# Sliding-window attention and SwiGLU on one core: the opening taken chunk by chunk, and x transposes two steps behind AV

## The chip, the cores and the metric

The kernel runs on one core of one Trainium2 chip. The metric is the device time of one execution in microseconds. Runs of the kernel before on the same chip stand beside every variant's runs, and all ratios are variant over before. PE is TensorE (matmul), PEld its weight load, ACT ScalarE, DVE VectorE, POOL GpSimd, SP SyncE. "Granted clock" is the share of full speed that the throttle gave to PE.

## The reference

```python
def _attn_ref(q, k, v):                      # B, H, S, D = 8, 8, 576, 64
    scores = (1.0 / np.sqrt(D)) * np.matmul(q, k.transpose(0, 1, 3, 2))
    rel = pos[:, None] - pos[None, :]
    scores = np.where((rel >= 0) & (rel < 64), scores, -1e9)   # window of 64, causal
    ...                                      # softmax over keys, then attn @ v
def reference(...):
    x = attn_out.transpose(0, 2, 1, 3).reshape(B * S, H * D)   # 4608 tokens x 512
    g = x @ w_gate; val = x @ w_val                            # 512 x 1536 each
    return (g * sigmoid(g) * val) @ w_out                      # 4608 x 512
```

## The kernel before

Tokens go in 36 chunks of 128. For a chunk n the steps are: transposes of k and q (`Tpe` on PE, `T` by DMA), scores and exponentials (`S`), attention times V (`AV`, with a division on VectorE that writes the tile `xb`), and the transpose of the result into `xT` (`X`, on PE, or by DMA if no engine is named). Four chunks make a group of 512 tokens. `F(c, f)` is one of the 12 blocks of gate and value matmuls of group c, optionally only columns lo to hi; `O(c, u)` is the output matmul of one chunk. V is needed twice, once shifted by 64 tokens across partitions: `shift_v` makes `vb` from `va`, either with two copies on an engine or with DMAs on SP's queue.

In every timeline below an engine's instructions stand in the order of these calls, and each waits for the semaphores of its inputs and buffers. So the order of the calls is each engine's queue. The kernel uses eight PSUM banks (the memory that PE writes to): `f` banks for F, one `o` bank for O, and `a` banks for the rest, each kind taken in rotation.

```python
    def opening(self):
        W = lambda a, b: (self.load_w("g", a, b), self.load_w("v", a, b))
        self.first_loads()                 # k and q of chunks 0, 1: one DMA each, on SP's and ACT's queue
        self.init()
        self.load(0, "v"); self.load(1, "v"); self.load(2, "kq")
        W(0, 1)
        self.load(2, "v"); self.load(3, "kqv")
        W(1, 2); W(2, 4); W(4, 6); ...
        self.warm(11)                      # dummy matmuls
        ... # casts and transposes of chunks 0 and 1 together
        self.S(0, True); self.S(1, True)
        self.shift_v(0, "dve"); self.shift_v(1, "dve")
        self.AV(0); self.Tpe(2, ("dve", "act")); self.AV(1)
        self.X(0, "act"); self.X(1, "dve")
        self.F(0, 0, 0, 256)
        self.banks("a", [5, 6, 7, 4])
        self.S(2, True); self.shift_v(2, "dve"); self.Tpe(3, ("dve", "act"))
        ...
        self.F(0, 1, 0, 256); self.AV(2)
        self.S(3, True); self.shift_v(3, "dve")
        self.F(0, 2, 0, 256); self.X(2, "act")
        self.F(0, 3, 0, 256); self.AV(3)
        self.F(0, 4, 0, 256); self.F(0, 5, 0, 256); self.X(3, "act")
        for f in range(6):
            self.F(0, f, 256, 512)
```

The softmax here doesn't subtract the row's maximum and nothing guards it: scores larger than these inputs give would overflow.

Of the kernel before, what the change touches and what calls it, by code (L numbers as in the profile page):

```python
# [17 lines left out]
BF = dt.bfloat16  # L18
# [131 lines left out]
class _Kernel:  # L150
# [15 lines left out]
    def alloc(self):  # L166
# [33 lines left out]
        f4 = lambda a: a.bitcast(F32).rearrange("p (h j d) -> p h j d", h=H, j=2)  # L200
        self.fk, self.fq = f4(hT[1][:, 0:2048]), f4(hT[1][:, 2048:4096])
        h1 = lambda a: [("hT", 1, f) for f in range(4 * a, 4 * a + 4)]
        self.fkk, self.fqk = h1(0), h1(1)
        c4 = lambda t: t[:, :].bitcast(BF).rearrange("p (j h d) -> p j h d", j=2, h=H)
        self.ck, self.cq = c4(self.ost[0]), c4(self.ost[1])
        self.ckk, self.cqk = [("ost", 0)], [("ost", 1)]
# [31 lines left out]
    def init(self):  # L238
        g = self.g
        self.zero(self.wup[:, :], ["wup"])  # L240
        g.op("act", lambda e: e.activation(self.wup[:, :], self.wup[:, :], ACTF.Exp), writes=["wup"])
        self.zero(self.ident[:, :], ["ident"])
        self.init_ident(self.ident, "ident")
        self.zero(self.wz[:, :], ["wz"])
        self.init_va(0, 4)
        self.zero(self.kT[:, :, 0:64], [("kT", -1, 0), ("kT", -1, 1)])
        self.zero(self.vb[0][0:64, :, 0:66], [("vb", 0, 0)])
        self.init_mask()
        for i in range(self.NP):
            self.zero(self.pt[i][:, :, 64:128], [("pt", i, 0), ("pt", i, 1)])  # L250
        self.init_va(4, self.NV)
# [42 lines left out]
    def shift_v(self, n, eng="sp"):  # L294
# [12 lines left out]
        for d, a, rk, wk in moves:  # L307
            if eng == "sp":
                g.op("sp", lambda e, d=d, a=a: e.dma_start(d, a), reads=rk, writes=wk, dma=True)
            else:  # L310
                self.copy(eng, d, a, rk, wk)
# [117 lines left out]
    def first_loads(self):  # L429
        for eng, x, dst, src, keys in (("sp", "k", self.fk, self.k, self.fkk), ("act", "q", self.fq, self.q, self.fqk)):  # L430
            d = dst.rearrange("p h j d -> p h (j d)")
            a = src[0, :, 0:256, :].rearrange("h (p j) d -> p h (j d)", j=2)
            self.g.op(eng, lambda e, d=d, a=a: e.dma_start(d, a), writes=keys, dma=True)

    def first_cast(self, x, eng, j):
        dst, src, keys, ck = (self.ck, self.fk, self.fkk, self.ckk) if x == "k" else (self.cq, self.fq, self.fqk, self.cqk)
        js = slice(j, j + 1) if j is not None else slice(0, 2)
        d = dst[:, js].rearrange("p j h d -> p h j d")
        wk = [("c", x, i) for i in range(2) if j in (None, i)]
        self.copy(eng, d, src[:, :, js], keys + ck, wk)  # L440

    def first_T(self, x, engs):
        g = self.g
        src = self.ck if x == "k" else self.cq
        for b in range(2):
            bank, bk = self.bank("a")
            tb = bank[:, 0:256].bitcast(BF).rearrange("p (c j t) -> p c j t", c=2, j=2)

            def pe(e, b=b, tb=tb):
                for j in range(2):  # L450
                    for c in range(2):
                        pr = 2 * b + c
                        r = e.transpose(tb[:, c, j, :], src[:, j, 2 * pr:2 * pr + 2, :], self.ident[:, :])
                return r

            rd = ["ident"] + [("c", x, j) for j in range(2)] + (self.ckk if x == "k" else self.cqk)
            g.op("pe", pe, reads=rd, writes=[bk])
            if x == "k":
                d = self.kT[:, 2 * b:2 * b + 2, 64:320]
                wk = [("kT", m, b) for m in (0, 1)]  # L460
            else:
                d = self.qT[:, 2 * b:2 * b + 2, 0:256]
                wk = [("qT", m, b) for m in (0, 1)]
            d = d.rearrange("p c (t j) -> p c t j", j=2)
            a = tb.rearrange("p c j t -> p c t j")
            self.copy(engs[b], d, a, [bk], wk)
# [66 lines left out]

    def hTk(self, ih):
        return [("hT", ih, f) for f in range(NF)] + [("hTp", ih, f, lo) for f in range(NF) for lo in (0, 256)]
# [46 lines left out]
    def opening(self):  # L582
        W = lambda a, b: (self.load_w("g", a, b), self.load_w("v", a, b))
        self.first_loads()
        self.init()
        self.load(0, "v")
        self.load(1, "v")
        self.load(2, "kq")
        W(0, 1)
        self.load(2, "v")  # L590
        self.load(3, "kqv")
        W(1, 2)
        W(2, 4)
        W(4, 6)
        self.load(4)
# [5 lines left out]

        self.banks("a", [0, 1, 2, 3, 5, 6, 7])
        self.warm(11)
        self.first_cast("k", "dve", None)
        self.first_cast("q", "act", 0)
        self.first_cast("q", "dve", 1)
        self.first_T("k", ("dve", "act"))
        self.first_T("q", ("dve", "act"))
        self.warm(2)
        self.S(0, True)  # L610
        self.S(1, True)
        self.shift_v(0, "dve")
        self.shift_v(1, "dve")
        self.AV(0)
        self.Tpe(2, ("dve", "act"))
        self.AV(1)
        self.X(0, "act")
        self.X(1, "dve")
        self.F(0, 0, 0, 256)
        self.banks("a", [5, 6, 7, 4])  # L620
        self.S(2, True)
        self.shift_v(2, "dve")
        self.Tpe(3, ("dve", "act"))
# [3 lines left out]
        self.load_wo(6, 12)  # L627
        for n in range(4, 8):
            self.shift_v(n)
        self.F(0, 1, 0, 256)  # L630
        self.AV(2)
        self.S(3, True)
        self.shift_v(3, "dve")
        self.F(0, 2, 0, 256)
        self.X(2, "act")
        self.F(0, 3, 0, 256)
        self.AV(3)
        self.F(0, 4, 0, 256)
        self.F(0, 5, 0, 256)
        self.X(3, "act")  # L640
        for f in range(6):
            self.F(0, f, 256, 512)
# [6 lines left out]
    def build(self):  # L649
        self.opening()  # L650
        self.Tpe(4, ("dve", "act"))
        self.F(0, 6)
        self.S(4)
        self.F(0, 7)
        self.AV(4)
        self.Tpe(5, ("dve", "act"))
        self.F(0, 8)
        self.X(4, "act")
# [3 lines left out]
        self.F(0, 10)  # L662
        self.X(5, "act")
        self.F(0, 11)
        self.Tpe(6, ("dve", "act"))
        self.Tpe(7, ("dve", "act"))
        for n in (8, 9, 10, 11):
# [3 lines left out]
        F1 = lambda *fs: [self.F(1, f, 0, 256) for f in fs]  # L671
        F1(0)
        self.S(6)
        F1(1, 2)
        self.AV(6)
        F1(3)
# [6 lines left out]
        self.X(7, "act")  # L683
        self.banks("a", [5, 6, 7])
        self.banks("o", [4])
        F1 = lambda *fs: [self.F(1, f, 256, 512) for f in fs]
        F1(0, 1)
        self.O(0, 0)
        self.S(8)
        self.load(12, after=8)  # L690
        F1(2, 3)
        self.AV(8)
        F1(4)
        self.O(0, 1)
        self.X(8, "act")
# [4 lines left out]
        self.AV(9)  # L700
        F1(7)
        self.X(9, "act")
# [3 lines left out]
        self.O(0, 2)  # L706
        self.AV(10)
        self.F(1, 8)
# [11 lines left out]
        self.O(0, 3)  # L720
# [66 lines left out]
```

## Time and profile before

| | before |
|---|---|
| time, median of 4 runs | 344.02 us (343.3 to 345.04) |
| span of the profiled run, granted clock | 341.6 us, 1.00 |
| first scores' mask matmul | 8.25 us |
| F behind x 3 starts | 25.0 us |
| scores of chunk 5 | 37.56 us |
| scores of chunk 13 | 92.70 us |

When PE reaches the scores of chunk 5, both versions have done exactly the same work: F(0,0) to F(0,8), chunks 0 to 4 through x, the transposes of chunk 5. The same holds at the scores of chunk 13. So differences there are pure gains or losses.

The view of busy time in stretches, of the kernel before; each engine has its busy us and count, and PEclk is the granted clock:

```profile
...
core 0: us, PE busy (x) PEld busy (x) DVE busy (x) ACT busy (x) POOL busy (x), PEclk, DMA share, GB/s
...
10.00:15.00 5.00, 3.45 (x63) 2.89 (x58) 2.99 (x11) 2.78 (x6) 5.00 (x7) 1.00 2.22 164
15.00:20.00 5.00, 4.73 (x77) 3.03 (x76) 4.03 (x12) 3.11 (x8) 5.00 (x8) 1.00 1.48 194
20.00:25.00 5.00, 4.08 (x52) 3.17 (x50) 4.75 (x14) 2.43 (x6) 5.00 (x8) 1.00 1.94 173
25.00:30.00 5.00, 5.00 (x46) 4.49 (x47) 4.19 (x10) 1.93 (x5) 5.00 (x8) 1.00 1.99 184
...
90.00:120.00 30.00, 30.00 (x251) 14.68 (x250) 20.78 (x45) 12.09 (x22) 8.26 (x10) 1.00 1.54 149
...
```

From 90 us on PE has no idle time. Whatever the change does must be done in the first 90 us.

The list of PE's waits of the kernel before, first from 5 to 25 us, then from 37 to 95 us ("x waits for y: us in total, times, longest"). L423 is the x transpose, L501 is F:

```profile
...
engine line waited for: us in total, times, longest us
PE ps L423 <- DVE xb L404: 1.0, 1, 1.0
...
PE ps L501 <- DVE uu L520: 0.7, 1, 0.7
PE ps L501 <- DVE xT L233: 0.5, 1, 0.5
PE ps L501 <- DMA Wv<-in_moe_w_val_dram: 0.5, 2, 0.3
...
```

```profile
...
PE ps L423 <- DVE xb L404: 2.3, 4, 1.3
PE ps L501 <- DVE uu L520: 0.7, 1, 0.7
...
```

In the opening no single wait exceeds 1.0 us. Later, most is 2.3 us that x transposes wait for `xb`, with AV's VectorE work just ahead of them.

How PE spends the time between the scores and AV of chunk 2, in its timeline (start, length, instruction):

```profile
...
15.46 0.41 PE L364 MATMUL ps<-qT,kT 64*128 64x64 bf16 x16
15.80 0.40 PE L477 MATMUL ps<-ident,kn 128*128 128x128 bf16 x4
...
16.35 0.61 PE L501 MATMUL ps<-xT,Wg 128*128 128x256 bf16 x4
16.92 0.61 PE L501 MATMUL ps<-xT,Wv 128*128 128x256 bf16 x4
17.37 0.19 PE L394 MATMUL ps<-vb,pt 128*128 128x65 bf16 x1
...
```

The scores (L364) start at 15.46 and AV (L394) at 17.37. The 1.9 us between them, in which ScalarE computes the exponentials, are filled with chunk 3's transposes (L477) and F(0,1).

### The profile page before, as it was taken

How to read it: one execution, taken by the hardware profiler on the slowest of the kernel's cores; microseconds unless marked ns; L12 is line 12 of the kernel's file. 1: busy time of each engine (PE TensorE's matmuls, PEld its weight loads, DVE VectorE, ACT ScalarE, POOL GpSimd, SP SyncE). 2: the span in 40 equal slices, each digit the busy share in tenths (PEclk: the TensorE clock that was granted, in tenths of full speed). 3: DMA queues.
4: the chain of work that ended last, by engine and by line, in shares of the span. 5: the costliest groups of instructions: out<-in, count | busy, mean ns of one | idle time of the engine just before them, and what ended most of it. 6: DMA issues, size and time to landing. Idle time of an engine off the chain costs nothing.

```text
span 341.6 us, 6841 instructions
## 1 busy us (share of the span) xinstructions
PE 330.3 (97%) x2705; PEld 172.2 (50%) x2705; DVE 222.5 (65%) x495; ACT 138.3 (40%) x252; POOL 111.8 (33%) x139
## 2 busy tenths in 40 slices
PE   7889998989999999999999999999999999999996
PEld 3567576654444444444444444444444444444444
DVE  8788987458666666666666666666666666655520
ACT  3555463355433333444333344444444443223221
POOL 8999760376322234333333334333300000000000
PEclk9999999999999999999999999999999999999999
DMA  9999999999999999999999999999953211100012
GB/s 177 172 183 185 182 207 159 173 194 200 183 152 143 140 146 145 142 145 141 141 140 136 153 138 139 131 141 141 129 141 93 76 48 46 49 31 33 31 59 96
DMA packets 174367, 44.93 MB, mean 132 GB/s; under 512 B 157888, under 2 KB 169856, under 8 KB 174336
## 3 DMA queue, kind: packets, MB, share of 16 engines
q0 software_dynamic: 118368, 18.36, 79.5%
q1 hardware_dynamic: 49744, 16.32, 29.2%
q10 hardware_dynamic: 6224, 9.83, 8.0%
q8 instruction: 21, 0.34, 0.5%
q14 instruction: 10, 0.08, 0.1%
HBM read 37.75 MB, written 9.44 MB: 138 GB/s over the span
## 4 chain that ended last, share of the span: by engine, by line
PE 86%; DVE 4%; POOL 3%; ACT 2%; DMA 2%; issue 1%; ACTq 0%; POOLq 0%
PE ps L501 50%; PE ps L547 27%; PE ps L364 3%; PE ps L394 2%; PE ps L395 2%; DMA Wv<-in_moe_w_val_dram 2%; DVE uu L520 2%; ACT pt L377 1%; POOL va L292 1%; DVE xb L404 1%; DVE hT L523 1%; PE ps L569 1%; POOL Wg L317 1%; PE ps L423 1%; POOL qn L292 1%
## 5 line engine op out<-in xcount | busy, mean ns | idle before, releaser
L520 DVE SCALAR_TENSOR_TENSOR uu<-sig,ps 128x512 bf16<-128x512 bf16 (+1 forms) x122 | 76.0, 623 | 86.7 <-ACT sig L512 85.9
L501 PE MATMUL ps<-xT,Wg 128*128 128x512 bf16 (+1 forms) x488 | 113.4, 355 | 1.9 <-DVE uu L520 1.4
L501 PE MATMUL ps<-xT,Wv 128*128 128x512 bf16 (+1 forms) x488 | 113.3, 355 | 0.5 <-DMA Wv<-in_moe_w_val_dram 0.5
L512 ACT ACTIVATE sig<-ps 128x512 bf16<-128x512 f32 (+1 forms) x122 | 66.9, 550 | 100.5 <-PE ps L501 100.5
L547 PE MATMUL ps<-Wo,hT 128*128 128x512 bf16 x420 | 96.1, 380 | 0.0
L523 DVE SCALAR_TENSOR_TENSOR hT<-uu,ps 128x512 bf16<-128x512 bf16 (+1 forms) x122 | 76.3, 626 | 4.2
L292 POOL DMA_DIRECT2D kn<-in_k_dram x38 | 33.4, 881 | 131.1 <-PE ps L364 126.3
L501 PEld LDWEIGHTS ps<-xT,Wv 128*128 128x128 bf16 x488 | 47.2, 98 | 47.2 <-DMA Wv<-in_moe_w_val_dram 0.8
L501 PEld LDWEIGHTS ps<-xT,Wg 128*128 128x128 bf16 x488 | 44.3, 98 | 40.6 <-ACT xT L231 1.7
L547 PEld LDWEIGHTS ps<-Wo,hT 128*128 128x128 bf16 x420 | 39.1, 98 | 44.5
L552 ACT ACTIVATE ost<-ps 128x512 f32<-128x512 f32 x35 | 20.9, 598 | 65.4 <-PE ps L547 65.4
L377 ACT ACTIVATE pt<-ps 128x512 bf16<-128x512 f32 x72 | 39.0, 596 | 18.7 <-PE ps L364 18.3
L292 POOL DMA_DIRECT2D va<-in_v_dram x40 | 35.7, 901 | 0.2 <-issue 0.2
L292 POOL DMA_DIRECT2D qn<-in_q_dram x38 | 33.6, 889 | 0.1
L404 DVE TENSOR_TENSOR xb<-ps,rc 128x256 bf16<-128x256 f32 x72 | 30.6, 425 | 2.5
L379 DVE TENSOR_TENSOR pt<-pt,mask 128x512 bf16<-128x512 bf16 x64 | 24.8, 420 | 8.0 <-ACT pt L377 7.5
L394 PE MATMUL ps<-vb,pt 128*128 128x65 bf16 x288 | 22.8, 193 | 0.4 <-DVE pt L379 0.2
L395 PE MATMUL ps<-va,pt 128*128 128x65 bf16 x288 | 22.8, 194 | 0.0
L394 PEld LDWEIGHTS ps<-vb,pt 128*128 128x128 bf16 x288 | 20.2, 98 | 4.6 <-DVE pt L379 1.2
L395 PEld LDWEIGHTS ps<-va,pt 128*128 128x128 bf16 x288 | 19.0, 97 | 3.3
L364 PEld LDWEIGHTS ps<-qT,kT 64*128 64x128 bf16 x576 | 10.4, 95 | 13.2 <-DVE rc L401 9.7
L364 PE MATMUL ps<-qT,kT 64*128 64x64 bf16 x576 | 14.7, 191 | 0.0
(47 smaller groups left out, 89.7 us busy)
## 6 DMA issues: line engine op xcount, KB each, us to landing
out_dram<-ost ACTq DMA_DIRECT2D x35, 256.0 KB, 4.9
vb<-va SPq DMA_DIRECT2D x63, 80.0 KB, 4.9
va<-in_v_dram POOLq DMA_DIRECT2D x32, 128.0 KB, 6.5
kn<-in_k_dram POOLq DMA_DIRECT2D x30, 128.0 KB, 4.5
qn<-in_q_dram POOLq DMA_DIRECT2D x30, 128.0 KB, 5.8
Wo<-in_moe_w_out_dram POOLq DMA_DIRECT2D x2, 768.0 KB, 14.9
Wg<-in_moe_w_gate_dram POOLq DMA_DIRECT2D x4, 256.0 KB, 7.0
Wv<-in_moe_w_val_dram POOLq DMA_DIRECT2D x4, 256.0 KB, 7.7
```

The lines of the kernel that those rows point to most:

```text
L292: self.g.op("pool", lambda e, d=d, a=a: e.dma_start(d, a), reads=gate, writes=ks, dma=True)
L364: r = e.matmul(sv[p][:, w, c], self.kT[ps, c, k0:k0 + 128], self.qT[ps, c, self.qs(n, 64 * w, 64 * w + 64)], start=not bias, stop=not bias ...
L377: g.op("act", lambda e, po=po, p=p: e.activation(po, sv[p], ACTF.Exp, scale=SCALE), reads=[bx[p][1]], writes=[pk])
L379: g.op("dve", lambda e, po=po: e.tensor_tensor(po, po, m, ALU.mult), reads=[pk, "mask"], writes=[pk])
L394: e.matmul(av[:, j, :], pt[:, h, 0:128], vb[:, h, 0:65], start=True, stop=False)
L395: r = e.matmul(av[:, j, :], pt[:, h, 64:192], va[:, h, 0:65], start=False, stop=True)
L404: g.op("dve", lambda e, xo=xo, av=av, rb=rb: e.tensor_tensor(xo, av[:, :, 0:64], rb, ALU.mult), reads=[bk, ("rc", ir)], writes=[("xb", ix, ...
L501: r = e.matmul(bank[:, lo:hi], W[:, kk, f * 128:f * 128 + 128], xT[:, kk, lo:hi], start=(kk == 0), stop=(kk == NK - 1))
L512: self.g.op("act", lambda e: e.activation(sig[:, lo:hi], G[:, lo:hi], ACTF.Tanh, scale=0.5), reads=[gk], writes=[("sig", i)])
L520: g.op("dve", lambda e: e.scalar_tensor_tensor(uu[:, lo:hi], sig[:, lo:hi], 1.0, G[:, lo:hi], ALU.add, ALU.mult), reads=[("sig", i), gk], ...
L523: g.op("dve", lambda e: e.scalar_tensor_tensor(hT[:, f, lo:hi], uu[:, lo:hi], 0.5, V[:, lo:hi], ALU.mult, ALU.mult), reads=[("uu", i), vk] ...
L547: r = e.matmul(OB[:, :], hT[:, f, 128 * u:128 * u + 128], self.Wo[:, f, :], start=(f == 0), stop=(f == NF - 1))
```

## The change

The intent: begin with chunk 0 alone instead of chunks 0 and 1 together, load V first, let ScalarE do V's shifts, hold W of F(0,1) back behind chunk 3, so that attention of the first chunks runs through early; and keep x transposes further behind AV. The diff, cut to its core:

```diff
 def init_...:
+        self.load(0, "v")                       # ahead of the identity matrix
-            self.zero(self.pt[i]...)            # all four on VectorE
+            # pt 0, 1 by copies on ScalarE, the rest on VectorE
-        self.init_va(4, self.NV)                # now at the end of the opening
 def opening:
-        self.first_loads()
+        self.first_loads(0); self.first_loads(1)       # a DMA per chunk for k and for q
...
         W(0, 1)
-        self.load(2, "v"); self.load(3, "kqv"); W(1, 2)
+        self.load(2, "vkq"); self.load(3, "vkq"); W(1, 2)
...
+        self.first_cast(0, "k", "dve"); self.first_cast(0, "q", "act")
+        self.Tpe(0, ("dve", "act")); self.warm(2); self.S(0, True)
+        self.first_cast(1, "k", "dve"); self.first_cast(1, "q", "dve")
+        self.shift_v(0, ("dve", "act")); self.Tpe(1, ("dve", "dve"))
+        self.AV(0)
+        self.S(1, True); self.shift_v(1, ("act", "act"))
+        self.X(0, "dve")
+        self.AV(1)
+        self.banks("a", [5, 6, 7, 4])
+        b0 = self.Fopen(); self.Fpart(b0, 0, 0, 0, 128)
+        self.Tpe(2, ("dve", "act")); self.X(1, "act")
+        self.Fpart(b0, 0, 0, 128, 256); self.Fclose(b0, 0, 0, 0, 256)
+        self.S(2, True); self.shift_v(2, ("act", "act")); self.shift_v(3)
+        self.AV(2)
+        self.Tpe(3, ("dve", "act"))
...
+        self.S(3, True); self.X(2, "dve")
+        self.F(0, 1, 0, 256); self.AV(3); self.F(0, 2, 0, 256); self.X(3, "act")
+        for f in range(3): self.F(0, f, 256, 512)
 def build:                                       # groups 0, 1
-        self.F(0, 10); self.X(5, "act"); self.F(0, 11)
-        self.Tpe(6, ...); self.Tpe(7, ...)
+        self.F(0, 10); self.Tpe(6, ...); self.X(5, "act"); self.F(0, 11)
...
-        F1(6, 7); self.X(7, "act"); ...; F1(0, 1); self.O(0, 0); self.S(8); F1(2, 3)
+        F1(6, 7); self.O(0, 0); self.X(7, "act"); self.O(0, 1); F1(0, 1, 2); self.S(8); F1(3)
         self.AV(8)
-        F1(4); self.O(0, 1); self.X(8, "act")
+        self.X(8); F1(4); self.O(0, 2)           # x 8 by DMA
...
         self.AV(9)
-        F1(7); self.X(9, "act"); self.S(10); self.O(0, 2); self.AV(10); self.F(1, 8)
+        self.X(9); F1(7); self.S(10); self.F(1, 8); self.AV(10); self.O(0, 3)   # x 9 by DMA
         self.X(10, "act")
```

More of the change, by code (lines that the diff above doesn't have):

```diff
@@ L199, in alloc @@
         self.ost = ring("ost", self.NO, DM, F32)
-        f4 = lambda a: a.bitcast(F32).rearrange("p (h j d) -> p h j d", h=H, j=2)
-        self.fk, self.fq = f4(hT[1][:, 0:2048]), f4(hT[1][:, 2048:4096])
-        h1 = lambda a: [("hT", 1, f) for f in range(4 * a, 4 * a + 4)]
-        self.fkk, self.fqk = h1(0), h1(1)
-        c4 = lambda t: t[:, :].bitcast(BF).rearrange("p (j h d) -> p j h d", j=2, h=H)
-        self.ck, self.cq = c4(self.ost[0]), c4(self.ost[1])
-        self.ckk, self.cqk = [("ost", 0)], [("ost", 1)]
+        f4 = lambda i: hT[1][:, 1024 * i:1024 * i + 1024].bitcast(F32)
+        self.fk, self.fq = [f4(0), f4(1)], [f4(2), f4(3)]
+        h1 = lambda i: [("hT", 1, 2 * i), ("hT", 1, 2 * i + 1)]
+        self.fkk, self.fqk = [h1(0), h1(1)], [h1(2), h1(3)]
         self.wup = sb("wup", 1, F32)
@@ L249, in init @@
         for i in range(self.NP):
-            self.zero(self.pt[i][:, :, 64:128], [("pt", i, 0), ("pt", i, 1)])
-        self.init_va(4, self.NV)
+            d, wk = self.pt[i][:, :, 64:128], [("pt", i, 0), ("pt", i, 1)]
+            if i < 2:
+                self.copy("act", d, self.wz[:, :].rearrange("p (h x) -> p h x", h=H), ["wz"], wk)
+            else:
+                self.zero(d, wk)
     def init_mask(self):
@@ L306, in shift_v @@
             moves.append((self.vb[i2][0:64], va[64:128], hi, [("vb", i2, 0)]))
-        for d, a, rk, wk in moves:
+        for j, (d, a, rk, wk) in enumerate(moves):
             if eng == "sp":
@@ L310, in shift_v @@
             else:
-                self.copy(eng, d, a, rk, wk)
+                self.copy(eng[j], d, a, rk, wk)
     def load_w(self, which, a, b):
@@ L427, in X @@
         self.copy(eng, xo, tb, [bk], [("xT", it, u)])
-    def first_loads(self):
-        for eng, x, dst, src, keys in (("sp", "k", self.fk, self.k, self.fkk), ("act", "q", self.fq, self.q, self.fqk)):
-            d = dst.rearrange("p h j d -> p h (j d)")
-            a = src[0, :, 0:256, :].rearrange("h (p j) d -> p h (j d)", j=2)
-            self.g.op(eng, lambda e, d=d, a=a: e.dma_start(d, a), writes=keys, dma=True)
-    def first_cast(self, x, eng, j):
-        dst, src, keys, ck = (self.ck, self.fk, self.fkk, self.ckk) if x == "k" else (self.cq, self.fq, self.fqk, self.cqk)
-        js = slice(j, j + 1) if j is not None else slice(0, 2)
-        d = dst[:, js].rearrange("p j h d -> p h j d")
-        wk = [("c", x, i) for i in range(2) if j in (None, i)]
-        self.copy(eng, d, src[:, :, js], keys + ck, wk)
@@ L442, in first_T, with first_loads @@
-    def first_T(self, x, engs):
-        g = self.g
-        src = self.ck if x == "k" else self.cq
-        for b in range(2):
-            bank, bk = self.bank("a")
-            tb = bank[:, 0:256].bitcast(BF).rearrange("p (c j t) -> p c j t", c=2, j=2)
-            def pe(e, b=b, tb=tb):
-                for j in range(2):
-                    for c in range(2):
-                        pr = 2 * b + c
-                        r = e.transpose(tb[:, c, j, :], src[:, j, 2 * pr:2 * pr + 2, :], self.ident[:, :])
-                return r
-            rd = ["ident"] + [("c", x, j) for j in range(2)] + (self.ckk if x == "k" else self.cqk)
-            g.op("pe", pe, reads=rd, writes=[bk])
-            if x == "k":
-                d = self.kT[:, 2 * b:2 * b + 2, 64:320]
-                wk = [("kT", m, b) for m in (0, 1)]
-            else:
-                d = self.qT[:, 2 * b:2 * b + 2, 0:256]
-                wk = [("qT", m, b) for m in (0, 1)]
-            d = d.rearrange("p c (t j) -> p c t j", j=2)
-            a = tb.rearrange("p c j t -> p c t j")
-            self.copy(engs[b], d, a, [bk], wk)
+    def first_loads(self, n):
+        for eng, dst, src, keys in (("sp", self.fk, self.k, self.fkk), ("act", self.fq, self.q, self.fqk)):
+            d = dst[n].rearrange("p (h d) -> p h d", h=H)
+            a = src[0, :, 128 * n:128 * n + 128, :].rearrange("h p d -> p h d")
+            self.g.op(eng, lambda e, d=d, a=a: e.dma_start(d, a), writes=keys[n], dma=True)
@@ L468, in Tpe, with first_cast @@
+    def first_cast(self, n, x, eng):
+        d, a, rk = (self.kn, self.fk, self.fkk) if x == "k" else (self.qn, self.fq, self.fqk)
+        self.copy(eng, d[n][:, :], a[n], rk[n], [(x + "n", n, 0), (x + "n", n, 1)])
     def Tpe(self, n, engs, what="kq"):
@@ L532, in F, with Fopen, Fpart, Fclose @@
         self.Fdve(c, f, i, G, gk, V, vk, lo, hi)
+    def Fopen(self):
+        return self.bank("f"), self.bank("f")
+    def Fpart(self, b, c, f, lo, hi):
+        self.Fmm(*b[0], self.Wg, "Wg", c, f, lo, hi)
+        self.Fmm(*b[1], self.Wv, "Wv", c, f, lo, hi)
+    def Fclose(self, b, c, f, lo, hi):
+        (G, gk), (V, vk) = b
+        i = self.Fact(G, gk, lo, hi)
+        self.Fdve(c, f, i, G, gk, V, vk, lo, hi)
     def hTk(self, ih):
@@ L583, in opening @@
         W = lambda a, b: (self.load_w("g", a, b), self.load_w("v", a, b))
-        self.first_loads()
+        self.first_loads(0)
+        self.first_loads(1)
         self.init()
-        self.load(0, "v")
         self.load(1, "v")
-        self.load(2, "kq")
         W(0, 1)
-        self.load(2, "v")
-        self.load(3, "kqv")
+        self.load(2, "vkq")
+        self.load(3, "vkq")
         W(1, 2)
-        W(2, 4)
+        W(2, 3)
+        W(3, 4)
         W(4, 6)
+        self.banks("a", [0, 1, 2, 3, 5, 6, 7])
+        self.warm(8)
+        self.first_cast(0, "k", "dve")
+        self.first_cast(0, "q", "act")
+        self.Tpe(0, ("dve", "act"))
+        self.warm(2)
+        self.S(0, True)
+        self.first_cast(1, "k", "dve")
+        self.first_cast(1, "q", "dve")
+        self.shift_v(0, ("dve", "act"))
+        self.Tpe(1, ("dve", "dve"))
+        self.AV(0)
+        self.S(1, True)
+        self.shift_v(1, ("act", "act"))
+        self.X(0, "dve")
+        self.AV(1)
+        self.banks("a", [5, 6, 7, 4])
+        b0 = self.Fopen()
+        self.Fpart(b0, 0, 0, 0, 128)
+        self.Tpe(2, ("dve", "act"))
+        self.X(1, "act")
+        self.Fpart(b0, 0, 0, 128, 256)
+        self.Fclose(b0, 0, 0, 0, 256)
+        self.S(2, True)
+        self.shift_v(2, ("act", "act"))
+        self.shift_v(3)
+        self.AV(2)
+        self.Tpe(3, ("dve", "act"))
         self.load(4)
@@ L600, in opening @@
         W(10, 12)
-        self.banks("a", [0, 1, 2, 3, 5, 6, 7])
-        self.warm(11)
-        self.first_cast("k", "dve", None)
-        self.first_cast("q", "act", 0)
-        self.first_cast("q", "dve", 1)
-        self.first_T("k", ("dve", "act"))
-        self.first_T("q", ("dve", "act"))
-        self.warm(2)
-        self.S(0, True)
-        self.S(1, True)
-        self.shift_v(0, "dve")
-        self.shift_v(1, "dve")
-        self.AV(0)
-        self.Tpe(2, ("dve", "act"))
-        self.AV(1)
-        self.X(0, "act")
-        self.X(1, "dve")
-        self.F(0, 0, 0, 256)
-        self.banks("a", [5, 6, 7, 4])
-        self.S(2, True)
-        self.shift_v(2, "dve")
-        self.Tpe(3, ("dve", "act"))
         self.load(6)
@@ L627, in opening @@
         self.load_wo(6, 12)
+        self.S(3, True)
+        self.X(2, "dve")
+        self.F(0, 1, 0, 256)
+        self.AV(3)
+        self.F(0, 2, 0, 256)
+        self.X(3, "act")
+        for f in range(3):
+            self.F(0, f, 256, 512)
+        self.init_va(4, self.NV)
         for n in range(4, 8):
             self.shift_v(n)
-        self.F(0, 1, 0, 256)
-        self.AV(2)
-        self.S(3, True)
-        self.shift_v(3, "dve")
-        self.F(0, 2, 0, 256)
-        self.X(2, "act")
-        self.F(0, 3, 0, 256)
-        self.AV(3)
-        self.F(0, 4, 0, 256)
-        self.F(0, 5, 0, 256)
-        self.X(3, "act")
-        for f in range(6):
-            self.F(0, f, 256, 512)
     def T8(self, n):
@@ L650, in build @@
         self.opening()
+        self.F(0, 3)
+        self.F(0, 4)
         self.Tpe(4, ("dve", "act"))
+        self.F(0, 5)
+        self.S(4)
         self.F(0, 6)
-        self.S(4)
+        self.AV(4)
         self.F(0, 7)
-        self.AV(4)
         self.Tpe(5, ("dve", "act"))
+        self.X(4, "act")
         self.F(0, 8)
-        self.X(4, "act")
         self.S(5)
@@ L662, in build @@
         self.F(0, 10)
+        self.Tpe(6, ("dve", "act"))
         self.X(5, "act")
         self.F(0, 11)
-        self.Tpe(6, ("dve", "act"))
+        F1 = lambda *fs: [self.F(1, f, 0, 256) for f in fs]
+        self.S(6)
+        F1(0, 1)
         self.Tpe(7, ("dve", "act"))
+        self.AV(6)
         for n in (8, 9, 10, 11):
@@ L670, in build @@
             self.T8(n)
-        F1 = lambda *fs: [self.F(1, f, 0, 256) for f in fs]
-        F1(0)
-        self.S(6)
-        F1(1, 2)
-        self.AV(6)
-        F1(3)
+        F1(2, 3)
         self.S(7)
@@ L682, in build @@
         F1(6, 7)
-        self.X(7, "act")
         self.banks("a", [5, 6, 7])
         self.banks("o", [4])
+        self.O(0, 0)
+        self.X(7, "act")
+        self.O(0, 1)
         F1 = lambda *fs: [self.F(1, f, 256, 512) for f in fs]
-        F1(0, 1)
-        self.O(0, 0)
+        F1(0, 1, 2)
         self.S(8)
         self.load(12, after=8)
-        F1(2, 3)
+        F1(3)
         self.AV(8)
+        self.X(8)
         F1(4)
-        self.O(0, 1)
-        self.X(8, "act")
+        self.O(0, 2)
         self.S(9)
@@ L700, in build @@
         self.AV(9)
+        self.X(9)
         F1(7)
-        self.X(9, "act")
         self.S(10)
@@ L705, in build @@
         self.T8(13)
-        self.O(0, 2)
+        self.F(1, 8)
         self.AV(10)
-        self.F(1, 8)
+        self.O(0, 3)
         self.X(10, "act")
@@ L719, in build @@
         self.load(17, after=12)
-        self.O(0, 3)
         self.F(1, 11)
```

## The prediction

> **What bounds the kernel now.** From about 84 us on PE is gapless: the view of busy time in stretches shows 20.00 us of PE in every 20 us at clock 1.00, the list of waits no PE wait after 100 us. So only the time up to 84 us can change. In the timeline real work on PE starts at 6.25 us (13 warm-up matmuls before do nothing), scores of chunk 0 at 8.25. From 8.25 to 25.0 PE has about 5 us of gaps: 1.2 and 0.7 around the x transposes of chunks 0, 1, 0.45 and 0.39 for W, 0.87 at the last x transpose. From 25 to 84 about 5 us, mostly an x transpose too close behind its AV: 0.5 at 41.9, 0.6 and 0.9 at 54 to 56, 0.4 at 69, 1.45 at 71.2, 0.5 at 82.3.
>
> **What the change does.**
> 1. Loads: k and q of chunks 0, 1 become four transfers of 1024 packets of 256 B instead of two of 1024 packets of 512 B. A 512 B packet takes 27 ns in the trace; k is delivered from 1.9 to 5.1 us, q from 3.2 to 5.6. The Trainium skill, "DMA: Bandwidth & Descriptors", Specifications, gives 512 B as the least size for line rate; no such 256 B load is in this trace. Estimate: k0 usable at 4.8 us, q0 5.3 to 6.3, q1 7 to 8.
> 2. Scores of chunk 0 start at 7.3 to 8.2: gain 0 to 0.9 us.
> 3. The chain gets longer: S1 waits for q1; V shifts of 64x640 go on ScalarE. By "ScalarE: Activation LUTs", What ACT_TABLE_LOAD costs (186 ns + 0.833 ns per element), one takes 0.72 us; the trace agrees for 128x512 (0.60). They stand behind the exponentials of chunks 1 and 2, ahead of AV1 and AV2: 0.7 to 1.6 us each. DVE saves 2.5 us of shifts and 0.87 us of memsets, not the limit there.
> 4. Chunks 2, 3 have little F work between their steps. Walking the queues with the trace's durations (scores to AV 1.8 us, AV to x 1.1, x copy 0.4 to 0.9) I get AV1 1.5 us later than before, the F work after X3 at 26 us (before 25.0), with three half-width F blocks (0.87 us each) fewer done. Opening: 2 to 4 us lost.
> 5. Later: X5 behind another transpose saves 0.5; X7 behind O(0,0) 1.4; X8, X9 on the DMA queue 0.44 of PE and the 1.45 and 0.4 waits. AV8 has less behind S8: 0.3 to 0.7 given back; DVE is nearly full from 30 to 57 us. Net gain 2.5 to 3.5 us.
>
> **Sum.** Losses and gains nearly cancel. My walk alone gives +0.5 to +1.5 us; it may be too pessimistic about landings, so I put 343.5 us, range 339 to 348. Faster by over 2% 0.09, within 2% 0.85, slower 0.06.
>
> **What would show it.** First scores at 7.3 to 8.2; PE gaps over 1 us before AV1 and AV2 released by ScalarE's V copies; F after X3 not before 25; hardly any wait for xb between 40 and 84 us; PE gapless from 84 us.
>
> **What would make it wrong.** The 256 B packets landing much earlier (up to 4 us faster), or q1 at 9 us or later (slower); a DVE backlog in the F blocks of group 1; late W; late DMA transposes of x 8, 9 stalling group 2.

## The result and the profile after

| | before | after |
|---|---|---|
| time, median of 4 runs | 344.02 us | 348.11 us (347.81 to 349.23) |
| ratio, with 95% interval | | 1.0122 (1.0088 to 1.0157) |
| granted clock of the four runs | 1.00 | 0.98 to 0.99 |
| first scores' mask matmul | 8.25 us | 7.10 us |
| F behind x 3 starts | 25.0 us | 28.3 us |
| scores of chunk 5 | 37.56 us | 43.42 us (+5.86) |
| scores of chunk 13 | 92.70 us | 97.17 us (+4.47) |

The kernel got 4.1 us slower, within 2%, but outside my range of 339 to 348 by 0.1 us.

The scores of chunk 5 in PE's timeline, first before, then after:

```profile
...
37.56 0.41 PE L364 MATMUL ps<-qT,kT 64*128 64x64 bf16 x16
...
43.42 0.41 PE L365 MATMUL ps<-qT,kT 64*128 64x64 bf16 x16
```

The same stretches of the kernel after, in the view of busy time in stretches:

```profile
...
10.00:15.00 5.00, 2.95 (x57) 2.13 (x56) 2.40 (x8) 3.06 (x6) 5.00 (x8) 1.00 2.36 157
15.00:20.00 5.00, 2.44 (x50) 1.78 (x50) 1.40 (x5) 3.52 (x7) 5.00 (x8) 1.00 1.70 196
20.00:25.00 5.00, 3.98 (x38) 2.50 (x37) 1.76 (x7) 2.06 (x4) 5.00 (x8) 0.53 1.93 173
25.00:30.00 5.00, 4.31 (x42) 3.49 (x40) 2.94 (x9) 1.56 (x4) 5.00 (x8) 0.78 1.95 176
...
```

Two things show. PE's busy time from 15 to 20 us fell from 4.73 to 2.44 us. And from 20 us the granted clock is 0.53, then 0.78, where it was 1.00 throughout before. Cut more finely, in the same view, the sparse stretch and the slow clock follow each other:

```profile
...
17.20:20.60 3.40, 1.11 (x24) 0.94 (x24) 1.28 (x6) 2.92 (x5) 3.40 (x6) 0.96 1.59 205
20.60:27.00 6.40, 5.92 (x53) 4.08 (x54) 2.67 (x8) 1.92 (x5) 6.40 (x9) 0.50 1.83 178
...
```

PE was busy for 1.11 of the first 3.4 us. In stretches of 0.1 us the same view puts the fall at 20.3 us, while PE was idle, and the return at 27.15, so PE ran at 0.50 for 6.8 us. (The expectations of e1 and e5 below put the fall at 20.7 us, 0.4 too late.) Two half-width F matmul groups in that time, in PE's timeline of the kernel after:

```profile
...
22.96 1.06 PE L473 MATMUL ps<-xT,Wg 128*128 128x256 bf16 x4
23.82 1.06 PE L473 MATMUL ps<-xT,Wv 128*128 128x256 bf16 x4
...
```

Gate and value (L473 is F now) start 0.86 us apart; before, from 16.35 to 16.92 and in the other half-width blocks that did not wait for W, it was 0.44 to 0.57 us.

What made PE sparse is in the list of its waits, 5 to 29 us, after (L395 is AV, L359 scores):

```profile
...
PE ps L395 <- ACT vb L228: 3.3, 2, 1.9
PE ps L473 <- ACT xT L228: 1.6, 2, 1.0
PE ps L359 <- DVE kT L230: 1.0, 1, 1.0
...
```

AV waited 3.3 us for ScalarE's `vb`, a wait that the list of before does not have. The timeline of PE from the scores of chunk 2 to its AV, and of ScalarE, both after:

```profile
...
16.09 0.59 PE L359 MATMUL ps<-nmask,ident 128*128 128x512 bf16 x2
16.62 0.41 PE L365 MATMUL ps<-qT,kT 64*128 64x64 bf16 x16
18.95 0.20 PE L395 MATMUL ps<-vb,pt 128*128 128x65 bf16 x1 [1.93 <-ACT vb L228]
...
```

```profile
...
10.47 1.08 ACT L378 ACTIVATE pt<-ps 128x512 bf16<-128x512 f32 x2 [0.53 <-PE ps L365]
11.56 1.50 ACT L228 ACTIVATE vb<-va 64x640 bf16<-64x640 bf16 x2
...
17.07 1.08 ACT L378 ACTIVATE pt<-ps 128x512 bf16<-128x512 f32 x2 [0.62 <-PE ps L365]
18.16 1.49 ACT L228 ACTIVATE vb<-va 64x640 bf16<-64x640 bf16 x2
```

PE has nothing between 16.62 and 18.95. The exponentials of chunk 2 run from 17.07 to 18.15; behind them in ScalarE's queue stand V 2's two shift copies (0.75 us each), and AV starts when the first of them is done. The same happened to chunk 1: exponentials at 10.47, shifts at 11.56, AV at 12.36. V 2 itself was in place by 12.05 us, where e12 below shifts it without waiting.

The list of PE's waits after, 37 to 100 us, answers to the second list of before:

```profile
...
PE ps L365 <- DVE xb L405: 0.7, 1, 0.7
...
PE ps L531 <- ACT ost L536: 0.5, 1, 0.5
PE ps L424 <- DVE xb L405: 0.4, 1, 0.4
...
```

The x transposes' 2.3 us went down to 0.4. But scores (L365) now wait 0.7 us for `xb` work, and O (L531) 0.5 us for ScalarE to empty its bank; both are new. From the scores of chunk 5 to those of chunk 13 the changed order is 1.39 us faster (5.86 less 4.47).

### The profile page after: what moved, and what is told of

The parts are those of the page before. It is cut to its first block, busy times and chain, and to the rows that moved or that the text cites. A ratio compares the mean times of both kernels' runs of the same rounds, so it can differ in the third digit from the quotient of the medians.

```text
span 346.0 us, 6749 instructions
## 1 busy us (share of the span) xinstructions
PE 329.1 (95%) x2636; PEld 171.0 (49%) x2678; DVE 218.4 (63%) x483; ACT 140.6 (41%) x252; POOL 112.8 (33%) x141
## 4 chain that ended last, share of the span: by engine, by line
PE 87%; ACT 5%; DVE 4%; issue 2%; DMA 1%; ACTq 0%
PE ps L473 50%; PE ps L531 27%; PE ps L365 3%; PE ps L395 2%; PE ps L396 2%; DVE uu L492 2%; ACT pt L378 2%; ACT sig L484 1%; DMA hT<-in_k_dram 1%; PE ps L449 1%; DVE xb L405 1%; PE ps L553 1%; PE ps L359 1%; ACT ost L536 1%; PE ps L424 1%
## 5 line engine op out<-in xcount | busy, mean ns | idle before, releaser
L473 PE MATMUL ps<-xT,Wg 128*128 128x512 bf16 (+2 forms) x468 | 111.5, 360 | 3.0 <-ACT xT L228 1.6
L473 PE MATMUL ps<-xT,Wv 128*128 128x512 bf16 (+2 forms) x465 | 112.7, 360 | 0.8
L484 ACT ACTIVATE sig<-ps 128x512 bf16<-128x512 f32 (+1 forms) x119 | 66.2, 558 | 100.4 <-PE ps L473 100.3
L531 PE MATMUL ps<-Wo,hT 128*128 128x512 bf16 x405 | 94.0, 380 | 1.9 <-issue 1.0
L473 PEld LDWEIGHTS ps<-xT,Wv 128*128 128x128 bf16 x480 | 46.9, 99 | 47.5
L473 PEld LDWEIGHTS ps<-xT,Wg 128*128 128x128 bf16 x480 | 43.7, 99 | 41.6 <-ACT xT L228 2.0
L531 PEld LDWEIGHTS ps<-Wo,hT 128*128 128x128 bf16 x420 | 39.1, 98 | 45.1 <-ACT ost L536 0.6
L395 PE MATMUL ps<-vb,pt 128*128 128x65 bf16 x288 | 23.3, 195 | 4.2 <-ACT vb L228 3.3
L395 PEld LDWEIGHTS ps<-vb,pt 128*128 128x128 bf16 x288 | 20.4, 99 | 9.4 <-ACT vb L228 3.6
L365 PEld LDWEIGHTS ps<-qT,kT 64*128 64x128 bf16 x576 | 10.6, 96 | 15.2 <-DVE rc L402 9.7
L365 PE MATMUL ps<-qT,kT 64*128 64x64 bf16 x576 | 14.9, 193 | 0.7 <-DVE xb L405 0.7
```

Source lines behind the costliest of these rows:

```text
L365: r = e.matmul(sv[p][:, w, c], self.kT[ps, c, k0:k0 + 128], self.qT[ps, c, self.qs(n, 64 * w, 64 * w + 64)], start=not bias, stop=not bias ...
L395: e.matmul(av[:, j, :], pt[:, h, 0:128], vb[:, h, 0:65], start=True, stop=False)
L473: r = e.matmul(bank[:, lo:hi], W[:, kk, f * 128:f * 128 + 128], xT[:, kk, lo:hi], start=(kk == 0), stop=(kk == NK - 1))
L484: self.g.op("act", lambda e: e.activation(sig[:, lo:hi], G[:, lo:hi], ACTF.Tanh, scale=0.5), reads=[gk], writes=[("sig", i)])
L531: r = e.matmul(OB[:, :], hT[:, f, 128 * u:128 * u + 128], self.Wo[:, f, :], start=(f == 0), stop=(f == NF - 1))
```

## The experiments

Sixteen kernels ran; all results were correct. The runs of many kernels fall into two groups 0.7 us apart, those of before near 343.4 and 344.1 us, those of e3 near 342.4 and 343.05; e14 and e15 show one group only. So differences under about 0.7 us are known only as averages: by the intervals, a difference between e3 and e13 or e14 is good to about 0.6 us either way. In the table, "clock" gives the granted clocks of the timed runs.

| run | ratio | median us | clock | verdict |
|---|---|---|---|---|
| e1 dummies in four waits | 1.0075 | 346.31 | 1.00 | clock is worth 1.6 us |
| e2 V shifts on VectorE | 1.0030 | 344.36 | five of six 1.00 | chain and clock |
| e3 later order alone | 0.9974 | 342.72 | 1.00 | gain 0.9 us |
| e4 opening alone | 1.0163 | 349.40 | 0.99 | loss 5.6 us |
| e5 dummies in one wait | 1.0066 | 346.69 | 0.99 to 1.00 | clock by chance |
| e6 F moved forward | 1.0093 | 346.96 | 0.99 to 1.00 | missed |
| e7 later order, x 8, 9 on PE | 1.0117 | 348.60 | 0.99 to 1.00 | test was spoilt |
| e8 later order rearranged | 1.0116 | 348.32 | 0.99 | my x 10 landed late |
| e9 e6 mended | 1.0001 | 344.05 | 1.00 | opening no gain |
| e10 e8 mended | 0.9920 | 340.93 | 1.00 | beats both |
| e11 before, x 8, 9 by DMA | 0.9964 | 342.37 | 1.00 | 1.2 us |
| e12 shifts ahead on ScalarE | 1.0021 | 344.67 | 0.995 or 1.00 | place, not engine |
| e13 e3, one wait off | 0.9950 | 341.80 | 1.00 | real loss |
| e14 e3, the other off | 0.9944 | 341.89 | 1.00 | real loss |
| e15 before, chunk 2's transposes later | 0.9982 | 343.17 | 1.00 | 0.6 us |
| e16 e12 with dummies | 1.0031 | 344.33 | 1.00 | splits the loss |

### e1: only the clock given back

```diff
         self.X(0, "dve")
+        self.warm(5)
         self.AV(1)
...
+        self.warm(3, b=2)
         self.Fpart(b0, 0, 0, 128, 256)
...
+        self.warm(7, b=2)
         self.AV(2)
         self.Tpe(3, ("dve", "act"))
+        self.warm(3, b=2)
```

> The changed kernel with 18 dummy matmuls put into PE's four longest waits of the opening (5 before AV of chunk 1, 3 before the second half of F(0,0), 7 before AV of chunk 2, 3 before the scores of chunk 3); every other instruction as in the changed kernel. Theory clock: the sparse PE work from 14 to 21 us made the granted clock fall to 0.50 from 20.7 to 27.1 us; with the dummies the clock stays 1.00, F after X3 starts at about 26.5 us instead of 28.3, and the time is 1.5 to 2.5 us under that of the changed kernel (ratio to before 1.005 to 1.008 instead of 1.0122). Rival chain: PE waited anyway, so a full clock changes less than 0.7 us (ratio 1.010 to 1.013).

Measured: ratio 1.0075, clock 1.00 in all five runs. The stretches that fell before, in the view of busy time in stretches of this run:

```profile
...
17.20:20.60 3.40, 3.09 (x34) 1.62 (x32) 1.28 (x6) 2.92 (x5) 3.40 (x6) 1.00 1.60 206
20.60:27.00 6.40, 4.44 (x63) 3.24 (x63) 3.37 (x10) 2.43 (x6) 6.40 (x9) 1.00 1.83 179
...
```

AV 2 starts at the same 18.95 us as in the changed kernel, so the chain is the same, but the scores of chunk 5 come at 41.70 instead of 43.42 us. The halved clock cost 1.7 us by the trace, 1.6 by the ratios (1.0122 less 1.0075, of 344 us). Doing more work on PE made the kernel faster. The rival, that a full clock changes less than 0.7 us, fell.

### e2: V shifts back on VectorE

```diff
-        self.shift_v(0, ("dve", "act"))   # and 1, 2: ("act", "act")
+        self.shift_v(0, ("dve", "dve"))   # and 1, 2: ("dve", "dve")
```

> The changed kernel with the V shifts of chunks 0, 1, 2 all back on VectorE; nothing else undone. If ScalarE's shifts behind the exponentials are what lengthens the chain: AV of chunk 1 about 1 us earlier than 12.4 us, AV of chunk 2 about 2 us earlier than 18.95, PE waits for ScalarE's vb copies (3.3 us) gone, and with the shorter gaps the clock may stay 1.00: 2 to 4.5 us under the changed kernel (ratio 1.000 to 1.006). If the chain is limited by something else (xb, qT, landings): under 1 us (ratio over 1.009).

Measured: 1.0030. AV 1 starts at 11.95 us (0.4 earlier, less than I expected), AV 2 at 17.84 (1.1 earlier, expected 2), scores of chunk 5 at 40.57. Part of the gain went elsewhere: chunk 1's scores came at 10.22 us instead of 9.49, since the copies of its transposes now stood behind V 0's shifts on VectorE. The clock stayed at 1.00 in five of six runs (0.995 once). Moving the shifts gave 3.2 us; if the clock is worth the 1.6 us of e1 here too, it is about half of that.

### e3 and e4: the two halves of the change

e3 is before's opening with the changed order from the x transpose of chunk 5 on, e4 the opposite.

> The opening of the kernel before, with the changed order only from the x transpose of chunk 5 on (x transposes two steps behind AV, x 8 and 9 transposed by DMA). My prediction said this part gains 2.5 to 3.5 us: ratio 0.990 to 0.993. Rival: the two traces, compared at the same point of the program, suggest a gain of only about 1.5 us (ratio 0.995 to 0.997) because the lateness moved to the waits of AV 8, S 10 and X 11.

> The changed opening with the order of before from the x transpose of chunk 5 on. If opening and later order simply add up, this run is slower than the changed kernel by what the run with the later order alone is faster than before: 1.5 us (ratio 1.016 to 1.018) or 2.5 to 3.5 us (1.019 to 1.023). If the later order helps only the changed opening, or only the old one, the two do not add up to 1.0122.

Measured: e3 0.9974, e4 1.0163. The later order gained 0.9 us alone, and 1.4 us when added to the changed opening (1.0163 less 1.0122). The opening lost 5.6 us. So the parts nearly add up, my 2.5 to 3.5 us for the later order was too much, and my 2 to 4 us for the opening too little. e3's trace shows the two new waits that the kernel after shows: by the list of waits 0.7 us before S 10 and 0.5 before O(0,1) (some expectations below say 0.9 and 0.6).

### e5: dummies in one wait only

```diff
+        self.warm(7, b=2)
         self.AV(2)
```

> The changed kernel with only the 7 dummy matmuls ahead of AV of chunk 2 (PE's 2 us wait from 17 to 19 us). If it is this sparse stretch just ahead of the fall at 20.7 us that costs the clock, the clock stays 1.00 and the whole gain of the 18 dummies is here: about 1.6 us under the changed kernel, ratio 1.007 to 1.009. If the sparseness over the whole of 10 to 20 us counts, the clock still falls and the ratio stays at 1.011 to 1.013.

Measured: 1.0066, but the runs differ: four at 1.00 took 346.1 to 346.7 us, one at 0.995 346.9, two at 0.99 348.3. In the profiled run, one of the two at 0.99, the clock was 0.50 from 14.4 to 21.2 us. It fell ahead of the dummies, behind a stretch in which PE was busy for 1.87 of 3.45 us. So neither expectation holds as written. With sparse stretches left, the clock fell in some runs of the same kernel and not in others, and when it did the run was about 2 us longer.

### e6 and e9: can the opening by chunks be mended?

```diff
 e6 = e2 and:
-        self.load(3, "vkq"); W(1, 2)
+        W(1, 2); self.load(3, "vkq")
...
+        self.F(0, 1, 0, 256)
         self.AV(2)
...      # F(0,2) ahead of AV(3); F(0,3), F(0,4) between AV(3) and X(3)
 e9 = e6 and:
         self.X(1, "act")
+        self.init_va(4, self.NV)                # was at the end of the opening
-        self.Tpe(3, ("dve", "act"))
+        self.Tpe(3, ("act", "act"))
```

> The changed kernel with V shifts on VectorE, and W of F(0,1) issued ahead of chunk 3 instead of behind it, so that F(0,1) fills PE's wait between scores and AV of chunk 2, and F(0,2), F(0,3), F(0,4) stand around AV and x of chunk 3. If what is left of the loss in the opening is PE work that the late W and the order withhold (0.85 us before AV 2, 1.07 us before x 3): 1.3 to 2 us under the run with V shifts on VectorE, ratio 0.997 to 0.999. If the later chunk 3 or W gives it back: ratio 1.002 to 1.006.

> The run with the F blocks of group 0 moved forward, which fell behind, with two things mended: the memsets of V's ones columns for chunks 4 to 9 go back ahead of the end of the opening (behind x 1, where VectorE is idle), since the DMA shift of V 4 waits for them and landed at 37.9 us with PE waiting 2.8 us; and both copies of chunk 3's transposes go on ScalarE, so that scores of chunk 3 do not wait for VectorE. If those two waits (and the clock falls that followed them) were what ate the gain: ratio 0.998 to 1.002. If the opening by chunks cannot keep PE dense enough: ratio over 1.005, clock below 1.00 in several runs.

Measured: e6 1.0093, a miss; e9 1.0001. In e6 PE waited 2.0 us before AV 4, which started at 37.9 us, and the clock fell twice in the profiled run. I had blamed this on V 4's DMA shift, which cannot start before the memsets that the change deferred to the end of the opening. With the memsets back ahead the wait was gone in e9 and the clock 1.00 in all five runs; since e9 also moves a copy, this points to the memsets but does not isolate them. Mended, the opening by chunks with the later order equals the kernel before, but its scores of chunk 5 still come at 39.65 us against 37.56: I found no version of this opening that pays.

### e7: x 8 and x 9 back on PE in the later order

```diff
-        self.X(8)
+        self.X(8, "act")                        # and X(9)
```

> The run with the later order alone, but x 8 and x 9 transposed on PE as before. My prediction put 0.44 us of PE work and 1.85 us of waits on these two; then this run is 1.5 to 2.3 us slower than with DMA transposes, ratio 1.002 to 1.004. If the waits only moved (to S 10, AV 10), it is 0.4 to 0.8 us slower: ratio 0.999 to 1.000.

Measured: 1.0117, far outside both. The test was spoilt: in the later order X(8) and X(9) stand directly behind AV, so on PE they waited 1.5 and 2.3 us for `xb`, and in four of six runs the clock was 0.990 to 0.995 as well. Its two runs at clock 1.00 took 345.7 and 346.4 us, still 1.7 and 2.4 us more than before. It only shows that this place needs the DMA.

### e11: x 8 and x 9 by DMA, nothing else

```diff
 (kernel before)
-        self.X(8, "act")
+        self.X(8)                               # and X(9)
```

> The kernel before, x 8 and x 9 by DMA transpose, nothing else changed. My prediction: 0.44 us of PE work and 1.85 us of waits come off, ratio 0.993 to 0.995. Rival: the wait for VectorE's AV work only moves from x 9 to the next instruction that needs its bank (S 10), ratio 0.997 to 0.999.

Measured: 0.9964, 1.2 us, between the two expectations. Where the rest went, in the PE timelines of the kernel before and of this run, at x 9 and S 10:

```profile
...
71.20 0.61 PE L501 MATMUL ps<-xT,Wv 128*128 128x256 bf16 x4
73.09 0.40 PE L423 MATMUL ps<-ident,xb 128*128 128x128 bf16 x4 [1.28 <-DVE xb L404]
...
```

```profile
...
70.65 0.61 PE L501 MATMUL ps<-xT,Wv 128*128 128x256 bf16 x4
71.99 0.38 PE L364 MATMUL ps<-qT,kT 64*128 64x64 bf16 x14 [0.72 <-DVE xb L404]
```

The transpose (L423) waited 1.28 us for `xb`. Without it, the scores of chunk 10 (L364) wait 0.72 us for the same VectorE work, since they need a PSUM bank that AV 9's division still reads.

### e8 and e10: the later order with its new waits taken away

```diff
 (e3, cut to what e8 and e10 share)
-        F1(6, 7); self.O(0, 0); self.X(7, "act"); self.O(0, 1)
+        F1(6); self.O(0, 0); self.X(7, "act"); F1(7); self.O(0, 1)
...      # F1(3, 4) ahead of AV(8)
-        F1(7); self.S(10); self.F(1, 8); self.AV(10); self.O(0, 3)
+        F1(7); self.F(1, 8); self.S(10); self.O(0, 3); self.AV(10)
...      # F(1, 9) to F(1, 11) one place later; opening: Tpe(2) behind X(1)
 e8:  x 10 by DMA, ahead of F(1, 9)
 e10: x 10 on PE, behind F(1, 9); Tpe(2) in banks 5, 6
```

> Kernel before's opening and the later order, with the new waits that the later order showed taken away: F(1,7) between x 7 and O(0,1) (0.63 us wait for the one O bank), F(1,8) ahead of the scores of chunk 10 (0.90 us wait for a bank that AV 9's VectorE work holds), F(1,3..4) ahead of AV 8, x 10 by DMA too; and in the opening the transposes of chunk 2 moved behind x 1, into the wait for its copy. If the waits are the reason why the later order gained only 0.9 us, they come off: 1.5 to 2.5 us under the later order alone, ratio 0.990 to 0.993. If they only move on: ratio 0.996 to 0.998.

> The rearranged later order on the opening of before again, but x 10 back on PE: its DMA transpose was issued at 82.8 us behind the queue's other work and landed at 91.6, with PE waiting 7.5 us for it. Also chunk 2's transposes take other PSUM banks, so that F(0,0) does not wait for their copies. If the waits for the O bank (0.63 us), for the bank of S 10 (0.90) and for x 1's copy really come off: 1.5 to 2.5 us under the later order alone (0.9974), ratio 0.990 to 0.993. If they move on: 0.995 to 0.998.

Measured: e8 1.0116, e10 0.9920. In e8 I had put x 10 on the DMA queue too. SP's queue was behind, in the timeline of SP and of PE of e8:

```profile
...
82.80 1.40 SPq L416 DMA_TRANSPOSE xT<-xb  x1
...
```

```profile
...
83.77 0.41 PE L364 MATMUL ps<-qT,kT 64*128 64x64 bf16 x16
91.70 1.87 PE L501 MATMUL ps<-xT,Wg 128*128 128x512 bf16 x4 [7.52 <-issue]
```

The transpose was issued at 82.80, though its `xb` was ready at 78.1, and landed 8.8 us later by the view of DMA issues. F(2,0) waited 7.5 us; the profile names no releaser, but the start at 91.70 fits the landing at 91.6. The clock then fell as well. With x 10 on PE, and the transposes of chunk 2 in other banks, the run is 2.7 us faster than before by the ratio (3.1 by the medians), the best of all, at clocks of 0.998 to 1.00. Its longest PE wait from 37 to 95 us is 0.5 us.

### e13, e14, e15: the edits of e10 one by one

```diff
 e13 (e3):  F1(6); self.O(0, 0); self.X(7, "act"); F1(7); self.O(0, 1)
 e14 (e3):  F1(7); self.F(1, 8); self.S(10); self.O(0, 3); self.AV(10); self.F(1, 9); self.X(10, "act"); ...
 e15 (before):  self.AV(0); self.AV(1); X(0), X(1); banks("a", [5, 6, 7, 4]); self.Tpe(2, ...); self.F(0, 0, 0, 256)
```

> The run with the later order alone, with one F block, F(1,7), put between x 7 and O(0,1), so that ScalarE has emptied the one O bank by then. If the 0.6 us wait is a real loss: 0.4 to 0.7 us under the later order alone, ratio 0.9955 to 0.9965. If the wait moves on to the next F blocks or AV 8: no change, 0.997 to 0.998.

> The run with the later order alone, with F(1,8) ahead of the scores of chunk 10 and the F blocks behind it one place later, so that VectorE has done AV 9 when chunk 10 needs its bank. If the 0.9 us wait is a real loss: 0.6 to 1.0 us under the later order alone, ratio 0.9945 to 0.9955. If it moves on to x 10 or AV 11: 0.9965 to 0.998.

> The kernel before with only the transposes of chunk 2 moved behind x 1 (and their PSUM banks): the trace of the combined run reached the scores of chunk 5 0.3 us earlier, so ratio 0.9985 to 0.9995; if the combined gain of 1.8 us was mostly this edit: under 0.996.

Measured: 0.9950, 0.9944, 0.9982. Against e3's 0.9974 the first wait was worth 0.8 us, the second 1.0 us, each good to about 0.6 us; the opening edit 0.6 against before. So both new waits were real losses, 1.8 us as a sum. In e10, which takes both off, less of it arrives: its 2.7 us less 0.6 for the opening edit leave 2.1 us for the later order, 1.2 more than e3. No run reached my 2.5 to 3.5.

### e12 and e16: the V shifts' place in ScalarE's queue

```diff
 e12 (after):
         self.AV(0)
+        self.shift_v(1, ("act", "act"))
         self.S(1, True)
-        self.shift_v(1, ("act", "act"))
...
         self.AV(1)
+        self.shift_v(2, ("act", "act"))          # was behind S(2)
 e16 = e12 and 9 dummies: 2 ahead of AV(1), 3 ahead of the second Fpart, 2 ahead of AV(2), 2 behind Tpe(3)
```

> The changed kernel with all V shifts where it has them by engine, but V 1's shift ahead of the scores of chunk 1 and V 2's right behind AV 1, so not behind the exponentials on ScalarE. If it is their place in ScalarE's queue, not the engine, that costs the chain: AV 2 about 1.1 us earlier than 18.95 us, AV 1 at most 0.4 us earlier, and 1.2 to 2 us under the changed kernel, or 3 us where the clock stays 1.00 (ratio 1.003 to 1.009). If the engine itself is to blame: ratio over 1.010.

> The changed kernel with V 1's and V 2's shifts moved ahead in ScalarE's queue, and 9 dummy matmuls in the waits that are left. Clock 1.00 in all runs expected; then the time is that of the three runs of the moved shifts whose clock was 1.00, 344.0 to 344.3 us, ratio 0.9995 to 1.001, and the loss of the change splits into 1.6 us of clock, about 2.3 us for the place of the shifts, and what is left of the chain against the gain of the later order. If the dummies cost time themselves: 1.002 to 1.004.

Measured: e12 1.0021. V's shifts stay on the same engine, with the same instructions. ScalarE's and PE's timelines of e12:

```profile
...
12.05 1.48 ACT L228 ACTIVATE vb<-va 64x640 bf16<-64x640 bf16 x2
...
16.31 1.08 ACT L378 ACTIVATE pt<-ps 128x512 bf16<-128x512 f32 x2 [0.62 <-PE ps L365]
...
```

```profile
...
15.86 0.41 PE L365 MATMUL ps<-qT,kT 64*128 64x64 bf16 x16
16.96 0.20 PE L395 MATMUL ps<-vb,pt 128*128 128x65 bf16 x1 [0.69 <-ACT pt L378]
...
```

Chunk 2's shifts now run at 12.05, ahead of its exponentials at 16.31, and AV 2 starts at 16.96, 2.0 us earlier than in the kernel after. AV 1 starts at 11.60, 0.8 us earlier, where I expected at most 0.4. The run is 3.5 us under the changed kernel, more than I expected: the clock fell in only half of the runs, and in the profiled one for 3.4 us, not 6.8. Its three runs at clock 1.00 took 344.0 to 344.3 us, the three at 0.995 about 345.1. e16 had 0.999 or 1.00 in every run. Four of its six runs took 344.1 to 344.4 us, as expected; two took 346.0 and 346.2, which makes the ratio 1.0031. The profile fell on one of these two: it reaches the scores of chunk 5 at 39.66 us, and has one PE wait of 2.0 us at 124 to 126 us, for the first F block of a later group. The list names VectorE's `hT`, but the x transpose that SP issued at 119.71 us landed 6.5 us later, at 126.2, and F started at 126.34; in e12, which has no such wait, the same transpose took 3.8 us. So I take it for a late DMA transpose; no run tests that.

With e1 and e16 at clock 1.00, the traces split the loss at the scores of chunk 5, here in the PE timelines of e1 and e16:

```profile
...
41.70 0.41 PE L365 MATMUL ps<-qT,kT 64*128 64x64 bf16 x16
...
39.66 0.41 PE L365 MATMUL ps<-qT,kT 64*128 64x64 bf16 x16
...
```

After 43.42, e1 41.70, e16 39.66, before 37.56 us: that is 1.7 us for the clock, 2.0 us for the place of the shifts of chunks 1 and 2, and 2.1 us for what is left of the opening. The times agree for the second part: e16's four undisturbed runs have a ratio of 1.0014, 2.1 us under e1's 1.0075.

## Why the prediction was right or wrong

Two steps of the prediction failed, both in size: "Opening: 2 to 4 us lost" left out the granted clock (point 4), and "Net gain 2.5 to 3.5 us" left out where the waits would move (point 5).

1. **What bounds the kernel.** Right. PE is gapless from 90 us before, and the difference at chunk 13, 4.47 us, is that of the spans, 4.4 us.
2. **Landings.** Right. The casts, which show by when data was usable, start at 4.62 us for k 0 (I said 4.8), 5.12 for q 0 (5.3 to 6.3) and 7.34 for q 1 (7 to 8). The first mask matmul starts at 7.10, a gain of 1.15 us where I had 0 to 0.9. (From run to run it shifts by some 0.4 us: 6.6 to 7.1 in the variants with the new loads, 8.2 to 8.7 in those with the old ones.) The Trainium skill, "DMA: Bandwidth & Descriptors", Specifications, which gives 512 B as the least size for line rate, was a fair warning: by the view of DMA, from 4.0 to 4.5 us, the k and q loads moved 287 GB/s, where the 512 B packets had moved 351.
3. **The longer chain.** Right in mechanism. ScalarE's shifts took 0.73 to 0.75 us (my estimate by the formula of the skill's "ScalarE: Activation LUTs", What ACT_TABLE_LOAD costs, was 0.72), stood behind the exponentials, and are the releaser of PE's two longest waits, 1.4 and 1.9 us. AV 1 came 1.3 us later than before (I said 1.5).
4. **"Opening: 2 to 4 us lost."** Mis-sized: 5.86 us at the scores of chunk 5. At clock 1.00 it is 4.1, the edge of my range. The other 1.7 us is a term that my sum did not have: the granted clock. I had listed gaps over 1 us before AV 1 and AV 2, and read them only as time in which PE waits. They also made PE sparse, and the work behind them ran at half speed: F behind x 3 started at 28.3 us instead of my 26. The skill's "TensorE: Matmul & The Clock Gate", Why this matters for your kernels, says to have no idle gaps over about 3 us. e8's wait of 7.5 us did bring the clock to 0.50. My gaps were shorter, 1.93 us at most, so I did not think of it; here the measurement decides.
5. **"Net gain 2.5 to 3.5 us" of the later order.** Mis-sized: 0.9 us alone, 1.4 us with the changed opening. The x waits came off as I said. But I took them off without asking which instruction would next need what VectorE was still working on. Two new waits, for O's bank and for the bank of S 10, gave 1.2 us (e10) to 1.8 us (e13 and e14 summed) back. I had given back only 0.3 to 0.7, before AV 8.
6. **The sum.** My walk said +0.5 to +1.5 us and I shaded it to -0.5 for a hope about landings. The first scores did come 0.2 us better than the walk's best case. The two mis-sized terms are each worth about 1.7 us, both on the slow side; they are the miss.

What stays open: how much the 128-column halves of F(0,0), the late W and the separate transposes each have in the remaining 2.1 us; and the exact condition for the clock's fall, which differs from run to run.

## What to carry to other kernels

A copy put on a less busy engine is not free if it stands in that engine's queue behind the work the next step waits for: moved ahead by a few calls, the same copies cost 2 us less here. When an order leaves PE sparse for a few microseconds, cost the clock too, and test it by filling the gaps with dummy matmuls. When you take a wait off, ask what needs the same buffer next, since the wait may only move one instruction on.

## What the Trainium skill lacked or had wrong

- "TensorE: Matmul & The Clock Gate", Why this matters for your kernels, gives idle gaps over about 3 us as what to avoid. Here the clock fell at 20.3 us with no idle time above 1.93 us since the opening's warm-up: PE was busy for 1.23 of the 3.45 us before. The page says in words, under "A second HAM failure mode: psum-queue depth-cycling", that frequent short idles of PE can do this too, but it has no figure for a window that is partly busy. The busy share alone does not decide it here: e12's clock fell at 19.1 us after 1.87 of 3.4 us, and the kernel before kept 1.00 with 1.85 of 3.4 us (11.7 to 15.1).
- The same page, Part 1, says the window runs freely and that results vary from run to run. The variation agrees: the same kernel (e5) took 346.1 to 346.7 us at clock 1.00 and 348.3 at 0.99. That a free window is the reason, no run here shows. Once fallen, the half clock lasted 6.8 us in the kernel after, e4 and e5, and 3.4 us in e12, so the cost of a fall is not fixed.
- "DMA: Bandwidth & Descriptors", Specifications, gives 512 B as the least for line rate. Its section "Why small descriptors are slow (HBM only)" gives an overhead for 256 B (27%), but no rate for such loads on the hardware queues. Here, with both queues running from 4.0 to 4.5 us: 287 GB/s, against 351 with 512 B.
- No page that I read has the time to landing of a DMA transpose on a queue in use: 3.3 and 4.7 us for x 8, 9 in the kernel after, 8.1 to 8.8 us in e8, where x 10's issue itself came 4.7 us after its data was ready.
